# A fused attention and two-layer kernel: batch 4's first layer moved into block form, twenty operand sums moved to GpSimd, another opening order

## The chip, the cores and the metric

The kernel runs on one core of a Trainium2 chip. The metric is the device time in microseconds of one execution; lower is better. The core has a matrix engine (TensorE, "PE" in the profile, with its weight loads as "PEld"), a vector engine (VectorE, "DVE"), an activation engine (ScalarE, "ACT"), GpSimd ("POOL"), a queue engine (SyncE, "SP") and 16 DMA engines. Each engine works through its own instructions in order, and semaphores tie them together.

## What is computed

The input holds q, k and v of 8 batches, 12 heads, 448 positions and 64 features, and two weight matrices. Cut to what matters:

```python
scores = np.matmul(q, k.transpose(0, 1, 3, 2)) / np.sqrt(64)
attn   = np.maximum(scores, 0.0) ** 2 / 448
x      = np.matmul(attn, v)            # per batch and head
x      = x.transpose(0, 2, 1, 3).reshape(8 * 448, 768)
h      = x @ w_in                      # 3584 x 768 times 768 x 2048
g      = 0.5 * h * (1 + erf(h / sqrt(2)))
out    = g @ w_out                     # 3584 x 2048 times 2048 x 768
```

The attention has no softmax: the scores are cut at zero and squared. Its output, with the heads side by side, is the input of a two-layer network with an exact GELU.

## The kernel before

**Attention.** A batch is 21 steps: three groups of four heads (g) by seven key blocks (i). A step is four score matmuls on quarters of the array (line 659), then relu with the scale from PSUM into an SBUF tile a_sq (line 671 on ScalarE, or line 673 on VectorE), then the square in place on VectorE (line 680, which reads the same SBUF tile as both operands). After seven steps of a group comes an attention product of 28 matmuls (line 720), whose PSUM tile is cast to the bfloat16 tile xT in two copies (L436 on VectorE or L438 on ScalarE). Scores, products and the block form's accumulators share three PSUM tiles ("w"); a_sq has 14 buffers.

**First layer.** In its plain form (`add_f1`, line 772) a batch is 16 chunks, each of six matmuls of 448 columns into one PSUM tile ("f", two of them) and one GELU on ScalarE (line 782). In its block form (`add_blocks`, `add_block`, line 916) weights and input are cut into 2 x 2 blocks, and seven products take the place of eight: 168 matmuls of 224 columns. For this VectorE makes sums of the input blocks (xs, line 883) and, once, sums of the weight blocks (ws, `add_wsums`, line 841, of which one is written over a part of the weights in place), and combines the products in passes from PSUM (line 950), before GELUs (line 959). Batches 0 to 4 use the plain form, 5 to 7 the block form.

**Second layer.** Its output is made in 14 groups of 256 rows. Group 0 is plain (line 1181). Groups 1 to 13 (`add_group`) use the same seven-product scheme: four sums s1 to s4 of pieces of h (line 1067, 1,024 elements per partition, each with one buffer), then seven products p1, p6, p2, p7, p5, p4, p3 of eight matmuls each (line 1086), with passes on VectorE or ScalarE (line 1120, and copies by 436 and 438), and stores by SyncE. h lives in a ring of two batches.

**Loads and transposes.** q and k of batches 2 to 7 come in by GpSimd's DMA queue and are turned by DMA transposes that SyncE issues (line 585, nine per batch). GpSimd works through one list (`pool_q`): loads, and before the loads of a later batch a small gate copy (line 626) that waits until the transposes of an earlier one have landed. The output weights are loaded behind such a gate.

**The order.** The program is laid out by a planner (class `Scheduler`). It knows an estimated duration and latency for each operation, and places operations one by one. The opening is written out by hand as a list (`ORDER`): each word is an engine's letter and an operation's number. TensorE's later order is a list too (`pe_q`): the attention of batches 2 to 7, with first-layer chunks and second-layer products (`flow`) spread between its steps in proportion, and after the attention the list `end`, with the block form of batches 5 to 7 and groups 7 to 13. The planner may pull a layer chunk forward by its own estimate. Operations with two possible engines get one from the planner. The order of each engine is fixed in the program; on the chip, an engine whose operands are late holds all that stands behind them.

`add_av` makes the attention product and its two casts, `F1B` and `GROUPS` say which batches' chunks and which groups go beside which attention batch.

Of the kernel before, what the change touches and what calls it, by code (L numbers as in the profile page):

```python
# [12 lines left out]
B, H, S, D = 8, 12, 448, 64  # L13
# [8 lines left out]
G = H // 4  # L22
# [4 lines left out]
KF = FF // 128  # L27
# [14 lines left out]
X_BIAS = -0.2  # L42
# [8 lines left out]
SWITCH = 0.09  # L51
# [3 lines left out]
SUM_BIAS = -0.3  # L55
TSUM_BIAS = 0.2
LEADS = {}
SHARES = (1.3, 1.0, 1.0, 1.0, 1.0, 1.0)
LAST = 256
PASSES = 5  # L60
# [20 lines left out]


ORDER = """
G0 D13 A10 P11 D12 A16 G1 P17 G2 P14 D18 D15 P42 P39 G3 P19 D43 P33 D20 P36 D44 P21 P23 A40 G4
A34 D22 P51 D41 D24 A37 P54 P25 A55 D26 D35 P48 G5 A52 G6 D56 A49 P57 P69 D38 G7 P63 G8 A58 G9
A64 P66 D70 P45 D53 D59 D50 G117 P27 D65 A67 A28 A47 P31 A46 G118 D68 P60 P81 D32 P29 D62 A61
A82 D30 P78 G119 D71 P108 G120 D109 P75 A79 P93 D83 G121 A76 D80 P72 P90 A94 D73 G122 A74 P96
P84 D95 A91 P129 P102 D110 D130 P131 A85 P141 A97 D92 D132 A103 G123 P156 D98 P105 P111 P143
A142 D77 A106 P165 D112 D86 A157 D113 A166 D107 P99 A100 P87 A89 D104 D101 D88 A144 P114 G124
D167 D115 G125 P159 A116 P162 P133 P249 A163 A160 G126 A250 G127 D134 D158 P171 G128 D164 P168  # L90
P174 A169 P135 A136 P145 P195 G147 D172 P183 A146 D175 G148 D173 P186 A187 P241 P251 S228 A184
D176 D161 D196 P189 P180 A242 A252 G149 A190 D188 G150 G151 P198 D170 S231 G152 D181 P137 P139
P192 P177 D138 A199 G153 A193 D140 D191 P207 P222 A178 D185 D208 P243 A223 S230 A179 P204 A244
A205 P216 D197 G154 D182 G155 S229 D194 D200 D224 A217 P213 D206 P245 A214 A246 P259 P219 P210
P201 A220 D209 A211 A260 P261 A262 D218 P263 P253 A264 A254 P255 A256 P257 S232 P247 A202 D215
A203 D221 D212 A258 P225 A248 P265
"""


# [14 lines left out]
class Scheduler:  # L114
# [168 lines left out]
    def place(self, fixed):  # L283


        fixed = {e: list(v) for e, v in fixed.items()}
        inside = {id(o) for v in fixed.values() for o in v}

        names = {"P": "PE", "A": "ACT", "D": "DVE", "G": "POOL", "S": "SP"}
        gone = set()  # L290
        for word in ORDER.split():
            op, eng = self.open[int(word[1:])], names[word[0]]
            _, dur, lat = next(e for e in op.engines if e[0] == eng)
            self.commit(max(self.ready(op), self.free[eng]), op, eng, dur, lat)
            gone.add(id(op))
        fixed = {e: [o for o in v if id(o) not in gone] for e, v in fixed.items()}
        rest = [o for o in self.open if id(o) not in inside | gone]
        while rest or any(fixed.values()):
            by = {}
            for o in rest:  # L300
                for e in o.engines:
                    w = by.setdefault(e[0], [])
                    if len(w) < self.WINDOW:
                        w.append(o)
            tops = [self.pick(v, e) for e, v in by.items()]
            for e, v in fixed.items():
# [13 lines left out]
def kernel(  # L320
# [9 lines left out]
    nc = tc.nc  # L330
# [101 lines left out]
    V, A = nc.vector, nc.scalar  # L432
# [25 lines left out]
    F1, F2 = {}, {}  # L458
# [162 lines left out]
    def add_gate(b, g):  # L621


        def fn(e):
            n = (16 * g + 1) * KC
            nc.gpsimd.tensor_copy(gate, get_T(b)[0][:, n : n + 16 * KC : KC])  # L626

        deps = [Tq[b, g, c][0] for c in range(NC)] + [Tk[b, g, 0][0]]
        pool_q.append(sch.add((("POOL", 0.2, 0.3),), fn, deps))
# [75 lines left out]
    def add_av(blk, bias):  # L705
        b, g, _, half = blk
        blocks = [(b, g, i, half) for i in range(NK)]
        w = S if half is None else HS
        pav = []

        def fn(e_):
            pav.append(w_pp.tile([128, 2, NB], F32, tag="w", name="pav"))
            for i in range(NK):
                for j in range(2):
                    r = slice(64 * j, 64 * j + 64)
                    for e in range(2):
                        o2 = 64 * (e ^ j)
                        n, y = (i, e) if b < 2 else divmod(NK * e + i, 2)
                        _, box, o = SQ[blocks[n]]
                        nc.tensor.matmul(  # L720
                            pav[0][o2 : o2 + 64, e, :w],
                            vt[b][r, 2 * g + e, bass.ts(i, D)],
                            box["a2"][r, y, o : o + w],
                            start=(i == 0),
                            stop=(i == NK - 1),
                        )

        deps = list(dict.fromkeys(SQ[x][0] for x in blocks)) + ld_v[b, g]

        last = {id(SQ[x][1]): x for x in SQ}  # L730
        gone = sum(last[id(SQ[x][1])] == x for x in blocks)
        d = 7 * 0.19 * w / S
        op = sch.add(
            (("PE", d, d + 0.24),), fn, deps, mode="A", bias=bias + AV_BIAS, need=("w",),
            frees=("a",) * gone,
        )
        AV[b, g, half] = op

        def get_x():
            if b not in xT:  # L740
                p, tag = (vpool, "v") if b in (B - 3, B - 1) else (xpool, "xT")
                xT[b] = p.tile([128, HP, S], BF16, tag=tag, name="xT")
            return xT[b][:, 2 * g : 2 * g + 2, cols(half)]

        old = [o for (bb, *_), o in F1.items() if bb == b - 2]
        if b == B - 2:
            old = [o for (bb, *_), o in F1.items() if bb == b - 3]
        if b in (B - 3, B - 1):
            old = [o for (bb, *_), o in AV.items() if bb == b - 1]
        xs = X[b, g, half] = []  # L750
        for j in range(2):
            xs.append(
                sch.add(
                    e_copy(w, 1), lambda e, j=j: copy(e, get_x()[:, j], pav[0][:, j, :w]),
                    [op] + old, frees=("w",), joint=list(xs), bias=bias + X_BIAS,
                )
            )
        xs[0].joint = [xs[1]]
# [68 lines left out]
        return t[:, :, 128 * m : 128 * (m + m1 - m0)]  # L827

    WS = {}

    def add_wsums(after, done):

# [25 lines left out]
    def add_blocks(b):  # L858
# [16 lines left out]

            return fn

        gone = [o for (bb, *_), o in QK.items() if bb == (B - 2 if b == B - 3 else B - 1)]

        def xsum(n, op, l, r, deps):  # L880
            return sch.add(
# [11 lines left out]
        for m4 in (0, M1 // 2):  # L893
            bank, todo = {}, []
            for y in range(2):
                ms = range(m4 + 2 * y, m4 + 2 * y + 2)
                todo.append(add_block(b, m4, y, ms, bank, x, t, TS, xs, old, half))
            for p in zip(*todo):
                atoms += [(0.58, o) for o in p]
            for name in ("a", "b", "c"):  # L900
                u, v = bank["end", name]
                u.joint, v.joint = [v], [u]
# [144 lines left out]
            queue.pop(0).dma_start(to[k, p0 : p0 + m, c], src[y : y + m, c])  # L1047
            j += m

    def add_group(g):  # L1050

        rows = [range(256 * g + 128 * x, 256 * g + 128 * x + 128) for x in range(2)]
        bs = sorted({r // S for t in rows for r in (t[0], t[-1])})
# [10 lines left out]
        def sum_op(n, op, a, b, deps):  # L1064
            def fn(e):
                box["s", n] = spool.tile([128, K2, 128], BF16, tag=f"s{n}", name=f"s{n}_sb")
                V.tensor_tensor(box["s", n], a(), b(), op=op)

            o = sch.add(
                (("DVE", 0.69, 0.8),), fn, deps, need=(f"s{n}",), bias=SUM_BIAS  # L1070
            )
            mine.append(o)
            return o

# [229 lines left out]
        add_load(2, g, g + 1)  # L1304
    add_steps(steps(1), ATT1_BIAS, True)
    add_T_dma(2, [[]] * 9)
    add_gate(2, G - 1)
    add_wout(0)
    add_wout(1)
    add_wout(2)  # L1310
    for m in range(0, HALF_M, 2):
        add_f1(0, m, 1, bias=F1B_BIAS)
    for m in range(HALF_M, KF):
# [20 lines left out]
    def at(b, n):  # L1334
        return [at_slot(b, n)]
# [1 line left out]
    for g in range(G):  # L1337
        add_load(3, g, g + 1)
    add_v(3, 0, G)
    flow, plans = [], {}  # L1340
    F1B = {2: 1, 3: 2, 4: 3, 5: 4}
    GROUPS = {2: (1,), 3: (2, 3), 4: (4, 5), 5: (6,)}
    for b in range(2, B):
        add_steps(steps(b), dve=True)
# [8 lines left out]
        if b + 1 < B:  # L1353
# [3 lines left out]
            if b + 2 < B:  # L1357
# [1 line left out]
                    add_gate(b + 1, g)  # L1359
                    add_load(b + 2, g, g + 1)  # L1360
                add_v(b + 2, 0, G)
        flow += [y for g in GROUPS.get(b, ()) for y in add_group(g)]
    add_wsums(at(B - 1, 1), [F1[B - 4, m, None] for m in range(KF)])

    def woven(x, y):

# [5 lines left out]
                out.append(y.pop(0))  # L1372
        return out + y

    end = woven(add_blocks(B - 3), add_group(7))
    end += add_group(8)
    end += woven(add_blocks(B - 2), add_group(9))
    g10 = add_group(10)
# [54 lines left out]
```

## Time and profile before

Three runs of the kernel took 370.72, 372.26 and 372.67 us; the median is 372.26. The profiled execution took 372.0 us, its span from the first to the last instruction is 370.2 us.

| engine | busy us | share of the span |
|---|---|---|
| PE | 359.3 | 97% |
| DVE | 279.0 | 75% |
| ACT | 205.5 | 55% |
| POOL | 63.4 | 17% |

The granted TensorE clock is 0.995 of full speed on average. The attention of batch 0 begins about 7 us after the start, that of batch 2 at 67, and the last attention product (batch 7) is at 252 us. From there to 365 us TensorE works on the block form and on groups 7 to 13.

In the profile's rows, "L680 DVE TENSOR_TENSOR a_sq<-a_sq 128x896 ... x88 | 51.8, 619 | 2.3" reads: line 680 of the kernel, on VectorE, writes tile a_sq from tile a_sq, 128 partitions by 896 elements, 88 times; busy 51.8 us in all, 619 ns each; the engine was idle 2.3 us just before them. A timeline row gives start, length, engine, line, operation, tiles and count. The rows of a timeline that have a count over one are merged instructions of the same kind in a row. Reported durations overlap slightly from one instruction to the next, so a pace is best taken from start to start.

### The profile page before, as it was taken

What the parts mean: (1) busy time and instruction counts of PE and PEld (TensorE: products, weight loads), DVE (VectorE), ACT (ScalarE), POOL (GpSimd) and SP (SyncE); (2) the same over time, 40 slices, a digit from 0 to 9 for tenths busy, and PEclk for the clock granted to TensorE, in tenths of its full rate; (3) what the DMA queues carried; (4) which work ended last, traced back from release to release, by engine and by line L of the source; (5) the groups of instructions that cost most, each with busy time, mean ns of one, the idle gap of its engine ahead of it and who ended that gap; (6) DMA issues with size and microseconds to landing.
All of it is one profiled execution on the core that took longest, in us unless ns stands there. A gap on an engine that the chain in (4) does not pass through costs nothing.

```text
span 370.2 us, 8463 instructions
## 1 busy us (share of the span) xinstructions
PE 359.3 (97%) x3557; PEld 222.2 (60%) x3557; DVE 279.0 (75%) x477; ACT 205.5 (55%) x315; POOL 63.4 (17%) x101
## 2 busy tenths in 40 slices
PE   7789999999999999999999999999999999999995
PEld 6566645455554455544455544457876897688663
DVE  3799930579997688997689978999878558755862
ACT  4798974664667745877755687854540353045200
POOL 8666301530023034004014000000000000000000
PEclk9899999999999999999999999999999999999999
DMA  9999997999999999999999993002002301210223
GB/s 171 195 201 203 202 200 115 161 203 196 200 140 228 164 160 177 171 153 210 164 156 183 201 180 76 2 0 88 2 0 87 88 0 43 90 41 2 85 85 87
DMA packets 89269, 47.27 MB, mean 128 GB/s; under 512 B 55312, under 2 KB 85776, under 8 KB 89232
## 3 DMA queue, kind: packets, MB, share of 16 engines
q0 software_dynamic: 32912, 22.47, 44.9%
q1 hardware_dynamic: 55952, 23.76, 36.3%
q8 instruction: 28, 0.46, 0.6%
q10 hardware_dynamic: 368, 0.51, 0.4%
q14 instruction: 9, 0.07, 0.1%
HBM read 45.61 MB, written 11.01 MB: 153 GB/s over the span
## 4 chain that ended last, share of the span: by engine, by line
PE 92%; ACT 3%; DVE 2%; DMA 1%; issue 0%; DVEq 0%
PE pso L1086 32%; PE psh L772 25%; PE pb L916 13%; PE ps L659 9%; PE pav L720 8%; ACT a_sq L671 3%; PE pso L1181 3%; DMA q<-in_q_dram 1%; PE tp L558 1%; DVE part L950 1%; PE tp L530 1%; DVE a_sq L680 0%; DVE xT L436 0%; ACT xT L438 0%; DVE kT L436 0%; DVE xs L883 0%
## 5 line engine op out<-in xcount | busy, mean ns | idle before, releaser
L671 ACT ACTIVATE a_sq<-ps 128x896 bf16<-128x896 f32 x139 | 120.0, 920 | 36.9 <-PE ps L659 36.9
L680 DVE TENSOR_TENSOR a_sq<-a_sq 128x896 bf16<-128x896 bf16 (+1 forms) x169 | 98.0, 616 | 3.0 <-ACT a_sq L671 2.0
L772 PE MATMUL psh<-xT,win_sb 128*128 128x448 bf16 (+1 forms) x516 | 96.4, 340 | 0.0
L772 PEld LDWEIGHTS <-win_sb 128*128 128x128 bf16 x516 | 47.9, 98 | 45.0 <-issue 9.1
L782 ACT ACTIVATE h_sb<-psh 128x448 bf16<-128x448 f32 x80 | 44.0, 550 | 26.9 <-PE psh L772 26.8
L1086 PEld LDWEIGHTS <-s_sb 128*128 128x128 bf16 x424 | 40.4, 98 | 27.5 <-issue 3.1
L673 DVE TENSOR_SCALAR a_sq<-ps 128x896 bf16<-128x896 f32 (+1 forms) x30 | 31.7, 1058 | 27.9 <-PE ps L659 27.9
L659 PE MATMUL ps<-qT,kT 64*64 64x448 bf16 (+1 forms) x756 | 48.0, 336 | 3.3 <-ACT a_sq L671 3.1
L950 DVE TENSOR_TENSOR part<-pb,part 128x448 f32<-128x448 f32 x60 | 34.6, 619 | 20.7 <-PE pb L916 20.7
L1086 PEld LDWEIGHTS <-h_sb 128*128 128x128 bf16 x312 | 29.9, 98 | 21.3 <-issue 2.8
L1086 PE MATMUL pso<-wout_sb,s_sb 128*128 128x384 bf16 (+2 forms) x216 | 38.1, 320 | 0.1
L1086 PE MATMUL pso<-wout_sb,h_sb 128*128 128x384 bf16 x208 | 38.1, 326 | 0.0
L1086 PE MATMUL pso<-t_sb,s_sb 128*128 128x384 bf16 x208 | 38.1, 326 | 0.0
L720 PE MATMUL pav<-a_sq,v_sb 64*64 64x448 bf16 (+1 forms) x756 | 37.3, 337 | 0.4 <-ACT a_sq L671 0.4
L659 PEld LDWEIGHTS <-kT 64*64 64x64 bf16 x756 | 18.3, 105 | 25.5 <-issue 19.5
L959 ACT ACTIVATE h_sb<-part 128x448 bf16<-128x448 f32 x36 | 20.1, 578 | 20.2 <-DVE part L950 20.0
L720 PEld LDWEIGHTS <-v_sb 64*64 64x64 bf16 x756 | 21.8, 110 | 11.9 <-issue 1.8
L916 PEld LDWEIGHTS <-win_sb 128*128 128x128 bf16 x288 | 27.6, 98 | 2.3 <-issue 0.4
L436 DVE CAST xT<-pav 128x448 bf16<-128x448 f32 (+1 forms) x38 | 21.1, 587 | 10.3 <-PE pav L720 9.7
L1120 DVE TENSOR_TENSOR osb<-pso,p_sb 128x384 f32<-128x384 f32 x39 | 21.7, 555 | 8.3 <-PE pso L1086 6.1
L626 POOL COPY gate<-qT 128x16 bf16<-128x16 bf16 x13 | 4.0, 304 | 110.1 <-DMA qT<-nq 110.1
L916 PEld LDWEIGHTS <-ws 128*128 128x128 bf16 x216 | 20.7, 98 | 0.0
(58 smaller groups left out, 291.3 us busy)
## 6 DMA issues: line engine op xcount, KB each, us to landing
nk<-in_k_dram POOLq DMA_DIRECT2D x23, 224.0 KB, 6.5
nq<-in_q_dram POOLq DMA_DIRECT2D x21, 224.0 KB, 9.1
v_sb<-in_v_dram POOLq DMA_DIRECT2D x5, 672.0 KB, 13.9
out_dram<-osb SPq DMA_DIRECT2D x8, 336.0 KB, 3.8
v_sb<-in_v_dram POOLq DMA_DIRECT2D x9, 224.0 KB, 8.5
out_dram<-osb SPq DMA_DIRECT2D x7, 288.0 KB, 3.4
out_dram<-osb SPq DMA_DIRECT2D x8, 240.0 KB, 3.1
win_sb<-in_moe_w_in_dram POOLq DMA_DIRECT2D x8, 192.0 KB, 8.6
```

The source lines that it names most:

```text
L436: V.tensor_copy(dst, src)
L659: nc.tensor.matmul(ps[64 * j : 64 * j + 64, e, x * w : x * w + w], kT[r, g, i * 128 + 64 * j : i * 128 + 64 * j + 64], moving, start=True, ...
L671: A.activation(ar, ps, AF.Relu, scale=c_att)
L673: V.tensor_scalar(ar, ps, c_att, 0.0, op0=mybir.AluOpType.mult, op1=mybir.AluOpType.max,)
L680: V.tensor_mul(box["a2"][:, :, :used], ar, ar)
L720: nc.tensor.matmul(pav[0][o2 : o2 + 64, e, :w], vt[b][r, 2 * g + e, bass.ts(i, D)], box["a2"][r, y, o : o + w], start=(i == 0), stop=(i == ...
L772: nc.tensor.matmul(ph[:, x * n : x * n + n], win_sb[:, kd, bass.ts(m + x, 128)], xT[b][:, kd, c], start=(kd == 0), stop=(kd == KD - 1),)
L782: A.activation(h_ring()[:, m : m + nm, o + c.start : o + c.stop], box[0][:, :S].rearrange("p (x n) -> p x n", x=nm), AF.Gelu,)
L916: nc.tensor.matmul(bank[name][:, y, z * HS : z * HS + HS], w[:, k, bass.ts(mm, 128)], right()[:, k], start=first and k == 0 and z == 0, st ...
L950: V.tensor_add(get(to), ps(name), get(other))
L1086: nc.tensor.matmul(box[bank][:, n0:n1], left()[:, kf], right()[:, kf, n0:n1], start=bool(need) and kf == 0, stop=kf == K2 - 1, skip_group_ ...
L1120: V.tensor_add(out()[:, n0:n1], box[bank][:, n0:n1], other()[:, n0:n1])
```

## The change

Three parts, which the planner's layout ties together:

1. Batch 4's first layer is made in block form too. Its 16 plain chunks leave the list beside attention batch 5, and its blocks come first in the list `end`, with no second-layer group woven in; the blocks of batch 5 and group 7 follow, as before. The tiles of the input sums take a buffer of the transposed keys of batch 6, and batch 6's own input sums follow in that buffer. The weight sums wait for the plain chunks of batch 3, the last plain ones now, and no longer for those of batch 4.
2. The four sums of each of groups 2 to 6, 20 in all, are made by GpSimd. They are put into its list: those of groups 2 and 3 after the loads of batch 5, those of groups 4, 5 and 6 after the loads of batch 7, which are its last.
3. The opening's list is another one. The planner now counts the time of a change between kinds of matmul while it follows that list, and takes the second cast of an attention product as dependent on the first. The loads of the output weights stand behind gates that wait for the first and the second third of batch 2's transposes, and the loads of batch 3 behind that for the last third; before, all stood behind the gate for the last third.

```diff
+POOLED = {2: 3, 3: 3, 4: 5, 5: 5, 6: 5}
...
 ORDER = """
-G0 D13 A10 P11 D12 A16 G1 P17 G2 P14 D18 D15 P42 P39 G3 P19 D43 P33 D20 P36 D44 P21 P23 A40 G4
...
+A10 P11 D13 A16 D12 P17 D18 P14 G0 P42 A15 G1 P39 A40 G2 P19 D43 G3 D44 P21 A22 P33 D20 P36 G4
...
@@ place
-            self.commit(max(self.ready(op), self.free[eng]), op, eng, dur, lat)
+            free = self.free[eng]
+            if eng == "PE" and self.mode not in (None, op.mode):
+                free += SWITCH
+            self.commit(max(self.ready(op), free), op, eng, dur, lat)
@@ add_av
-                    [op] + old, frees=("w",), joint=list(xs), bias=bias + X_BIAS,
+                    [op] + old + xs, frees=("w",), joint=list(xs), bias=bias + X_BIAS,
@@ add_blocks
-        gone = [o for (bb, *_), o in QK.items() if bb == (B - 2 if b == B - 3 else B - 1)]
+        gone = [o for (bb, *_), o in QK.items() if bb == (B - 2 if b == B - 4 else B - 1)]
+        if b == B - 2:
+            gone += blocks[B - 4]
...
+                blocks.setdefault(b, []).extend(p)
@@ add_group
-    def add_group(g):
+    def add_group(g, pooled=None):
...
-                V.tensor_tensor(box["s", n], a(), b(), op=op)
-
-            o = sch.add(
-                (("DVE", 0.69, 0.8),), fn, deps, need=(f"s{n}",), bias=SUM_BIAS
-            )
+                (V if pooled is None else nc.gpsimd).tensor_tensor(box["s", n], a(), b(), op=op)
+
+            eng = ("DVE", 0.69, 0.8) if pooled is None else ("POOL", 2.3, 2.5)
+            o = sch.add((eng,), fn, deps, need=(f"s{n}",), bias=SUM_BIAS)
+            if pooled is not None:
+                pooled.append(o)
@@ the main list
-    add_gate(2, G - 1)
+    add_gate(2, 0)
     add_wout(0)
     add_wout(1)
+    add_gate(2, 1)
     add_wout(2)
+    add_gate(2, 2)
...
-    flow, plans = [], {}
-    F1B = {2: 1, 3: 2, 4: 3, 5: 4}
+    flow, plans, held = [], {}, {}
+    F1B = {2: 1, 3: 2, 4: 3}
...
-        flow += [y for g in GROUPS.get(b, ()) for y in add_group(g)]
-    add_wsums(at(B - 1, 1), [F1[B - 4, m, None] for m in range(KF)])
+        flow += [y for g in GROUPS.get(b, ()) for y in add_group(g, held.setdefault(g, []) if g in POOLED else None)]
+        for g in POOLED:
+            if g in held and POOLED[g] == b:
+                pool_q.extend(held[g])
+    add_wsums(at(B - 1, 1), [F1[B - 5, m, None] for m in range(KF)])
...
-    end = woven(add_blocks(B - 3), add_group(7))
+    end = list(add_blocks(B - 4))
+    end += woven(add_blocks(B - 3), add_group(7))
```

More of the change, by code (lines that the diff above doesn't have):

```diff
@@ L83 @@
 ORDER = """
-G0 D13 A10 P11 D12 A16 G1 P17 G2 P14 D18 D15 P42 P39 G3 P19 D43 P33 D20 P36 D44 P21 P23 A40 G4
[L85 to L96, printed above, removed]
+A10 P11 D13 A16 D12 P17 D18 P14 G0 P42 A15 G1 P39 A40 G2 P19 D43 G3 D44 P21 A22 P33 D20 P36 G4
+P54 G5 P25 A37 P23 A55 G6 P51 D34 P48 A24 A49 D26 D35 D56 D41 D38 A52 P69 D70 G7 P57 P63 A58
+D53 P45 D50 P66 G8 G9 D59 A64 A46 P27 P31 D28 G117 D32 A67 D65 D68 A47 G118 P60 P78 G119 A61
+P29 D30 G120 P81 A79 A82 D62 G121 G122 P93 A94 D71 P108 P84 A85 P75 D109 A76 D83 D80 P72 P90
+D73 P129 D95 P105 A74 G123 P102 A91 D130 A106 P131 D86 D77 G124 D132 P141 D92 A103 P111 P96
+G125 A112 P165 P143 A97 D104 P156 D107 A166 A157 P87 D113 D98 P99 D110 D88 G126 A142 D89 P114
+P174 P133 D100 G127 A101 A175 D115 D116 P159 A144 P168 D134 G128 P171 D169 A160 P135 D172 D173
+D170 A136 G147 P251 P192 D193 P186 P162 A252 P145 D176 A163 A146 P243 P253 P180 P195 A187 A244
+P198 P137 A254 G148 D164 D158 P139 G149 G150 A181 D167 G151 A199 D161 P183 D196 A184 P177 D138
+D140 D188 G152 P189 P219 P245 P247 D194 A178 A190 S231 A220 D185 A179 P207 P216 A246 S229 D182
+P213 D191 D197 P261 A248 A208 S232 P263 S228 D200 A214 P222 D217 P204 D221 D209 P201 D215 A262
+A223 A264 P210 A211 P265 G153 S230 A266 P259 A260 P249 P255 D218 D205 A202 A250 A203 P257 D224
+G154 A256 D206 D212 P225 P267 G155 A258
 """
@@ L829 @@
     WS = {}
+    blocks = {}
     def add_wsums(after, done):
```

## The prediction

> **What bounds the kernel now.** I read the page first. The parts on busy time and on slices:
>
> ```profile
> PE 359.3 (97%) x3557; PEld 222.2 (60%) x3557; DVE 279.0 (75%) x477; ACT 205.5 (55%) x315; POOL 63.4 (17%) x101
> ...
> PE   7789999999999999999999999999999999999995
> ...
> DVE  3799930579997688997689978999878558755862
> ...
> POOL 8666301530023034004014000000000000000000
> ```
>
> TensorE is busy in every slice but the first three and the last: about 11 of 370.2 us are idle, and the chain that ended last is 92% PE. So every microsecond of matmul taken away counts, provided that the engines feeding it keep up. VectorE is the one near its limit: 9 tenths in many slices of the attention. GpSimd is nearly free, and after 200 us empty.
>
> Then the timeline of PE, for the pace of the two forms of the first layer (start, us, line, count):
>
> ```profile
> 48.37 6.98 PE L772 MATMUL psh<-xT,win_sb 128*128 128x448 bf16 x36
> 55.28 0.95 PE L720 MATMUL pav<-a_sq,v_sb 64*64 64x448 bf16 x16
> ...
> 306.72 1.31 PE L916 MATMUL pb<-xs,win_sb 128*128 128x224 bf16 x12
> 307.87 1.31 PE L916 MATMUL pb<-xT,ws 128*128 128x224 bf16 x12
> ```
>
> From start to start, 36 plain matmuls take 6.91 us (0.192 each) and 12 block ones 1.15 us (0.0958 each), with no gap between groups.
>
> Then VectorE's groups between 105 and 230 us, where groups 2 to 6 of the second layer lie, with the engines' busy time in that stretch:
>
> ```profile
> L680 DVE TENSOR_TENSOR a_sq<-a_sq 128x896 bf16<-128x896 bf16 x88 | 51.8, 619 | 2.3 <-ACT a_sq L671 1.5
> L673 DVE TENSOR_SCALAR a_sq<-ps 128x896 bf16<-128x896 f32 x14 | 15.3, 1092 | 12.6 <-PE ps L659 12.6
> L436 DVE CAST xT<-pav 128x448 bf16<-128x448 f32 x25 | 14.4, 616 | 1.2 <-PE pav L720 1.1
> L1067 DVE TENSOR_TENSOR s_sb<-h_sb 128x1024 bf16<-128x1024 bf16 x10 | 6.8, 683 | 0.0
> ...
> 105.00:230.00 125.00, 124.88 (x1172) 63.43 (x1171) 105.28 (x177) 84.89 (x120) 22.48 (x37) 1.00 1.24 172
> ```
>
> The stretch's columns are PE, weight loads, DVE, ACT, POOL. VectorE is busy 105.3 of 125 us. Its most frequent operation is the square, which reads two operands from SBUF; relu, the casts to xT and the passes read PSUM.
>
> Last, how late the squares may be (timelines of DVE and PE around an attention product of the last batch):
>
> ```profile
> 231.47 1.27 DVE L680 TENSOR_TENSOR a_sq<-a_sq 128x896 bf16<-128x896 bf16 x2
> ...
> 233.18 1.49 PE L720 MATMUL pav<-a_sq,v_sb 64*64 64x448 bf16 x28
> ```
>
> The last square ends at 232.74, the product starts at 233.18: 0.44 us to spare. Over the 18 products of batches 2 to 7 the same difference is 0.2 to 2.4 us, 1.05 on average; they come every 10 us.
>
> **The Trainium skill.** "GPSIMD Engine Reference", section 3.1, gives about 2.6 cycles per element at 1.2 GHz for a two-input tensor_tensor. Estimate for 1,024 elements: 2.2 us. The trace of before has no such operation on GpSimd. "SBUF — State Buffer", section "Who interferes with whom", says that a VectorE instruction with two SBUF inputs contends with a GpSimd instruction that reads SBUF, and that whichever starts first holds the shared port for its whole instruction. The trace agrees for one direction. Two gate copies on GpSimd with what VectorE did meanwhile:
>
> ```profile
> 143.52 0.61 POOL L626 COPY gate<-qT 128x16 bf16<-128x16 bf16 x1 [9.36 <-DMA qT<-nq]
> ...
> 143.44 0.62 DVE L680 TENSOR_TENSOR a_sq<-a_sq 128x896 bf16<-128x896 bf16 x1
> ...
> 169.56 0.21 POOL L626 COPY gate<-qT 128x16 bf16<-128x16 bf16 x1 [0.89 <-DMA qT<-nq]
> ...
> 168.90 1.09 DVE L673 TENSOR_SCALAR a_sq<-ps 128x896 bf16<-128x896 f32 x1 [1.29 <-PE ps L659]
> ```
>
> Under a square the copy takes 0.61 us and ends 0.07 after the square; under a relu from PSUM it takes 0.21. Seven of the 13 copies fall under a two-input operation, and each ends 0.06 to 0.08 after it; the other six take 0.2. The opposite direction, VectorE held by GpSimd, no run here shows yet.
>
> **The change, part by part**, against the profiled execution's own 372.0 us (span 370.2, so 1.8 around it; the median of the runs shown is 372.26, 0.3 above, which I neglect).
>
> *Batch 4 in block form.* Removed: 16 chunks of 6, 96 x 0.192 = 18.4 us of PE. Added behind the attention: 168 matmuls (504 in three batches now) x 0.0958 = 16.1. Sum **-2.3 us**, on the path, as PE is full there. Added on DVE: 20 passes of 0.62 and 4 sums xs of 0.5, 14.4 us beside 16.1 of PE; the first blocks now have no second-layer group woven in. Now VectorE spends 7.2 of 10 us in 260 to 270 and PE doesn't wait; each bank's pass has a pair of products (1.15 us) as cover, against 0.62. Taken as 0; if the weight sums (8 x 0.95) come late too, VectorE passes 16.1 us and it costs up to 2. ACT: 16 GELUs as before and 4 copies (0.53), hidden, since it is busy 5 of 10 us there.
>
> *Attention made shorter.* PE loses 18.4 us of filler, so the same squares, relus and casts must be done in 18.4 us less. In the stretch above: DVE 105.3 less the 20 sums on GpSimd (start to start 0.6 each, 12) is 93 in 106.6 us, 87% against 84% before. ACT: 84.9 less 16 GELUs x 0.55 is 76 in 106.6, 71%. Loads and transposes per batch must also be done in some 26 instead of 30 us; SP's transposes of one batch started 22 us after those of the batch before at the fastest (113.6, then 135.6), so they fit.
>
> *The 20 sums on GpSimd.* Each takes 2.2 us by the page's price; bounds: 1.1 (the 128-element affine select takes 0.31 and the 16-element copy 0.20, so about 1 ns an element) and 2.8 (a 0.6 us wait for a square in front). For 20 it is 45 us in which GpSimd reads SBUF. What does VectorE do meanwhile? It goes on until the next two-input operation stands at its head. Without the sums 92 of 157 of its operations in the stretch are of that kind (88 squares and 4 sums xs and ws), 59%; so it gets through 0.41/0.59 = 0.7 operations of about 0.7 us, 0.5 us, and stands for the remaining 1.7. Times 20: 35 us (0 if it isn't held at all). Against it: the 13.6 us that VectorE has idle in the stretch, and the slack of about 1 us in front of an attention product, once for each of the five groups, 5 us. Remainder 35 - 13.6 - 5 = 17 us of PE waiting. I take **+12**: the planner sees a lighter VectorE, may place relus on ACT (14 of 1.09 us are on VectorE in the stretch, ACT has 30 us idle; five moved give 5 us). Ends: -0 and +22.
> What waits in VectorE's queue behind a held square is all of it: the relu and the two casts that give PSUM tiles back to the next scores, the passes that free a bank for the next product, and the last square of an attention product; PE's order is fixed, so it waits too.
> What waits behind the sums in GpSimd's queue: those of groups 2 and 3 stand ahead of the gates of batch 5 and the loads of batch 6. The sums of group 3 need the buffers that group 2's products give back, near the end of batch 4. So these loads, at 147 to 172 us now, start about one third of a batch or more later; they have the length of batch 5 (26 us) until their first scores. 4.1 MB at 200 GB/s is 20 us, transposes follow by thirds: hidden, with some 8 us to spare. Behind the sums of groups 4 to 6 stands nothing.
>
> *Gates and output weights.* The first gate now waits for a third of batch 2's transposes, so the weight loads (63.8 now) go out some 10 us earlier and share the DMA engines with the other transposes (all done at 61; the first scores of batch 2, at 67, need the first third alone). Two more gate copies, 0.2 us each on a GpSimd that waits there: 0; if the later thirds slip by more than some 10 us, up to +1.
>
> *Opening and planner.* The order lists engine by engine nearly the same work; PE is idle 4.5 us between 6 and 30 us, in waits of 0.4 us for a relu. The planner now counts mode switches there and puts the second cast behind the first. Bounds -1.5 and +1.5; taken as 0.
>
> Sum: 372.0 - 2.3 + 12 = **381.7, so 382 us**.
>
> **Rivals.**
> *A, forecast: VectorE is held* (above), 376 to 391. For it: the copies of 0.61 us. Chance 0.62.
> *B, held but absorbed*: the held time is under (13.6 + 5)/20 = 0.9 us per sum or a little more, because GpSimd gives the port back early or the sums fall where VectorE casts. Then 371 to 376, mostly 373. Chance 0.14.
> *C, the other side: VectorE isn't held by GpSimd's reads, or under 0.9 us a sum, and the shorter matmuls arrive whole*: 372.0 - 2.3 = 369.7, with the opening's bounds 368.3 to 371. For it: PE idles nowhere else, and 84 to 87% of VectorE was enough. Against: the copies show that reads exclude each other. Chance 0.17.
> *D, GpSimd's queue*: the loads of batch 6 or a sum are late and PE waits for DMA or for GpSimd itself. Between p5 of one group and p6 of the next lie p4, p3 and p1, 3.9 us and attention; two sums take 4.4. At 2 us for each of the three such seams and up to 8 us for late transposes, 372.0 - 2.3 + 6 to 14 gives 376 to 384. Chance 0.07, as the cause on its own.
>
> **From these to the numbers.** About 0.5% (1.9 us) is what a measurement of this kernel can tell from no change. Faster, under 370.4: C, 0.17 plus a little of B, 0.18. Within: part of B and the edge of C, 0.09. Slower: A, D and half of B, 0.73. The range 369.3 to 390 takes in half of C, all of B and D and nine tenths of A, some 0.83; A alone is 376 to 391.
>
> **What would show it.** Squares on line 680 longer than 0.63 us or gaps before them, while a sum of 2 us or more runs on GpSimd; PE waiting for VectorE between 110 and 235 us, where it has no wait now, in steps at groups 2 to 6; the end of attention at about 251 - 18 + 12 = 245 us, and the tail after it 16 us longer than now at the same pace. C would show the end of attention at 233 and squares at 0.62. Wrong would make it: sums of 1.1 us; a planner that empties VectorE at those places; squares that go on under a sum.

## The result and the profile after

The changed kernel takes 401.6 us (median of four runs, 397.2 to 409.1), the kernel before 372.2 beside it: a ratio of 1.076, with a 95% interval of 1.066 to 1.085 (the ratio leaves out the run of 409.1 us, which fell in a slower state). The forecast was 382 us, with a range up to 390. The sign was right, the size wrong by a factor of three: +29.4 us instead of +10.

The page after, parts on busy time and slices (the profiled execution's span is 399.3 us):

```profile
PE 366.6 (92%) x3629; PEld 231.3 (58%) x3629; DVE 305.4 (76%) x484; ACT 204.3 (51%) x316; POOL 110.2 (28%) x123
...
PE   8699999999999839799979879899999999999995
...
DVE  3999814898987708998799979998979766765862
...
POOL 8755212401123096901390817200000000000000
PEclk9999999999999969899989969999999999999999
```

TensorE, full in every slice before, now has seven holes between slices 14 and 26, and four of them (15, 17, 21 and 23) lie where GpSimd's row has an 8 or a 9. Its busy time went up by 7.3 us although its work went down by 2.3; the row of the granted clock says why: it has 6 and 8 there, where before it had 9.

Where in the run the time goes can be read from PE's timeline: the start of each batch's first score matmul, of the first block-form product, and the end (us).

| kernel | b=2 | b=3 | b=4 | b=5 | b=6 | b=7 | first block product | end |
|---|---|---|---|---|---|---|---|---|
| before | 67.1 | 102.6 | 132.7 | 162.8 | 192.0 | 222.9 | 251.6 | 370.2 |
| after | 65.0 | 97.6 | 125.5 | 167.0 | 194.2 | 225.8 | 263.5 | 399.3 |

Up to batch 4 the change is 7 us ahead, as a thinner filler should make it. Then batch 4 takes 41.5 instead of 30 us, batch 7 37.6 instead of 29. By the first block product it is 11.8 us behind, where 18.4 ahead was the plan: 30.2 us are lost in the attention. What follows takes 135.9 instead of 118.6 us, 17.3 more, against 16.1 for the matmuls added there.

The three largest of PE's waits, none of which was there before (us in total, times, longest):

```profile
PE pso L1095 <- POOL s_sb L1075: 8.4, 1, 8.4
PE pav L724 <- DVE a_sq L684: 7.4, 7, 1.9
PE pso L1095 <- DVE osb L1129: 3.9, 3, 2.3
```

And one place of the second kind in full, group 5's sums in batch 7 (timelines of GpSimd, VectorE and TensorE):

```profile
223.50 2.39 POOL L1075 TENSOR_TENSOR s_sb<-s_sb,h_sb 128x1024 bf16<-128x1024 bf16 x1
225.84 2.50 POOL L1075 TENSOR_TENSOR s_sb<-h_sb 128x1024 bf16<-128x1024 bf16 x1
228.31 2.49 POOL L1075 TENSOR_TENSOR s_sb<-h_sb,s_sb 128x1024 bf16<-128x1024 bf16 x1
...
224.29 1.07 DVE L677 TENSOR_SCALAR a_sq<-ps 128x896 bf16<-128x896 f32 x1
225.28 6.00 DVE L684 TENSOR_TENSOR a_sq<-a_sq 128x896 bf16<-128x896 bf16 x3
231.20 0.54 DVE L1129 TENSOR_TENSOR osb<-pso,osb 128x384 f32<-128x384 f32 x1
...
228.88 0.57 PE L724 MATMUL pav<-a_sq,v_sb 64*64 64x448 bf16 x8 [1.75 <-DVE a_sq L684]
231.33 0.89 PE L724 MATMUL pav<-a_sq,v_sb 64*64 64x448 bf16 x7 [1.88 <-DVE a_sq L684]
...
233.69 2.74 PE L1095 MATMUL pso<-t_sb,s_sb 128*128 128x384 bf16 x8
```

Three squares, which take 1.7 us in a row with no sum beside them, take 6.0: while GpSimd sums, VectorE's square stands, gets in between two sums, and the next one stands again. The relu from PSUM at 224.29, under a sum too, takes its usual 1.07. PE waits for the squares, and the product that follows takes 2.74 us instead of 1.46: half clock.

### The profile page after: what moved, and what is told of

The parts are those of the page before. It is cut to its first block, busy times and chain, and to the rows that moved or that the text cites. A ratio compares the mean times of both kernels' runs of the same rounds, so it can differ in the third digit from the quotient of the medians.

```text
span 399.3 us, 8659 instructions
## 1 busy us (share of the span) xinstructions
PE 366.6 (92%) x3629; PEld 231.3 (58%) x3629; DVE 305.4 (76%) x484; ACT 204.3 (51%) x316; POOL 110.2 (28%) x123
## 4 chain that ended last, share of the span: by engine, by line
PE 66%; DVE 15%; SPq 6%; ACT 5%; DMA 4%; issue 2%; POOL 2%; DVEq 0%; POOLq 0%; ACTq 0%
PE pso L1095 24%; PE pb L924 14%; PE psh L776 14%; DVE a_sq L684 8%; SPq L589 6%; PE ps L663 6%; PE pav L724 5%; DMA qT<-nq 4%; ACT a_sq L675 4%; DVE part L958 2%; DVE osb L1129 1%; DVE a_sq L677 1%; PE spin L1256 1%; DVE ws L846 1%; POOL s_sb L1075 1%
## 5 line engine op out<-in xcount | busy, mean ns | idle before, releaser
L675 ACT ACTIVATE a_sq<-ps 128x896 bf16<-128x896 f32 x131 | 113.4, 918 | 59.6 <-PE ps L663 59.4
L684 DVE TENSOR_TENSOR a_sq<-a_sq 128x896 bf16<-128x896 bf16 (+1 forms) x169 | 116.8, 733 | 3.0 <-ACT a_sq L675 2.3
L776 PE MATMUL psh<-xT,win_sb 128*128 128x448 bf16 (+1 forms) x420 | 77.9, 339 | 0.0
L958 DVE TENSOR_TENSOR part<-pb,part 128x448 f32<-128x448 f32 x80 | 46.1, 620 | 22.2 <-PE pb L924 22.2
L776 PEld LDWEIGHTS <-win_sb 128*128 128x128 bf16 x420 | 39.1, 98 | 36.6 <-issue 9.1
L677 DVE TENSOR_SCALAR a_sq<-ps 128x896 bf16<-128x896 f32 (+1 forms) x38 | 40.8, 1075 | 22.9 <-PE ps L663 22.8
L1095 PE MATMUL pso<-t_sb,s_sb 128*128 128x384 bf16 x208 | 41.5, 347 | 10.1 <-POOL s_sb L1075 8.4
L786 ACT ACTIVATE h_sb<-psh 128x448 bf16<-128x448 f32 x64 | 35.0, 550 | 23.2 <-PE psh L776 23.1
L967 ACT ACTIVATE h_sb<-part 128x448 bf16<-128x448 f32 x48 | 26.7, 578 | 25.4 <-DVE part L958 25.1
L1075 POOL TENSOR_TENSOR s_sb<-h_sb 128x1024 bf16<-128x1024 bf16 x10 | 23.5, 2350 | 26.9 <-PE pso L1095 26.8
L924 PEld LDWEIGHTS <-ws 128*128 128x128 bf16 x288 | 27.6, 98 | 0.4 <-issue 0.4
## 6 DMA issues: line engine op xcount, KB each, us to landing
win_sb<-in_moe_w_in_dram POOLq DMA_DIRECT2D x8, 192.0 KB, 8.5
```

The source lines that it names most:

```text
L675: A.activation(ar, ps, AF.Relu, scale=c_att)
L677: V.tensor_scalar(ar, ps, c_att, 0.0, op0=mybir.AluOpType.mult, op1=mybir.AluOpType.max,)
L684: V.tensor_mul(box["a2"][:, :, :used], ar, ar)
L776: nc.tensor.matmul(ph[:, x * n : x * n + n], win_sb[:, kd, bass.ts(m + x, 128)], xT[b][:, kd, c], start=(kd == 0), stop=(kd == KD - 1),)
L786: A.activation(h_ring()[:, m : m + nm, o + c.start : o + c.stop], box[0][:, :S].rearrange("p (x n) -> p x n", x=nm), AF.Gelu,)
L924: nc.tensor.matmul(bank[name][:, y, z * HS : z * HS + HS], w[:, k, bass.ts(mm, 128)], right()[:, k], start=first and k == 0 and z == 0, st ...
```

## The experiments

**The sums back on VectorE.** Edit:

```diff
-POOLED = {2: 3, 3: 3, 4: 5, 5: 5, 6: 5}
+POOLED = {}
```

> The changed kernel with all second-layer sums on VectorE again; block form of batch 4 and the new opening stay. Theory 'hold' (GpSimd's reads of the sums keep VectorE's two-operand instructions waiting) and theory 'queue' (the sums come late because of what stands before them in GpSimd's list) both expect the whole loss gone: 366 to 370 us, that is 372.2 less 2.3 for the block form and about 2 for the opening; no square over 0.65 us. Theory 'thin filler' (with 18 us of matmul gone from beside the attention VectorE can't follow, wherever the sums are) expects 380 us or more.

382.9 us, ratio 1.028 (1.021 to 1.035). So taking the sums back gains 18.7 us, and the rest, which was forecast as a gain of 2.3, costs 10.8. The size that "thin filler" named came, but not its mechanism. Timelines of VectorE, TensorE and SyncE of this kernel:

```profile
166.62 0.56 DVE L1129 TENSOR_TENSOR osb<-pso,p_sb 128x384 f32<-128x384 f32 x1 [6.98 <-DMA out_dram<-osb]
...
167.23 2.72 PE L1095 MATMUL pso<-t_sb,h_sb 128*128 128x384 bf16 x8 [5.55 <-DVE osb L1129]
...
152.78 3.42 SPq L589 DMA_TRANSPOSE kT<-nk  x1
156.26 4.60 SPq L589 DMA_TRANSPOSE qT<-nq  x2
160.97 2.41 SPq L1055 DMA_DIRECT2D out_dram<-osb  x4
```

VectorE isn't overloaded here, it stands idle for 7 us. It wants an output tile (there are three), and the store that frees it goes out at 161, behind transposes of batch 5 that take SyncE up to 3.4 us each, though group 2's output was complete at 151.7. From 165.4 us on, still within PE's wait, the clock is at half for 6.8 us: the 16 matmuls after the wait take 5.1 us instead of 2.6.

**The three parts alone, on the kernel before.** The sums alone (group 4's ahead of the last v load, since the planner has no solution otherwise; group 7's, on VectorE, are planned after them):

```diff
+POOLED = {2: 3, 3: 3, 4: 5, 5: 5, 6: 5}
...
+                if g == 4:
+                    pool_q[-1:-1] = held[g]
+                else:
+                    pool_q.extend(held[g])
```

> The kernel before with only the 20 sums of groups 2 to 6 on GpSimd (group 4's stand before the last v load, as the plan has no solution otherwise; group 7's are planned after them). Hold: 20 us of longer squares as in the changed kernel, some of it absorbed as the filler is 18 us thicker: 385 to 400 us. Queue: only the one wait of 8 us at group 2, if the gates of batch 4 are as late: 380. Thin filler: 372 to 376.

411.2 us, ratio 1.100 (1.091 to 1.108), above what any theory said. In its profiled execution, the longest of the four with 414.2 us, PE waited 13.0 and 11.7 us for the second sum of groups 2 and 4, both behind gates in GpSimd's list, and squares were 17 us longer in all. The sums cost more here than in the changed kernel, so the parts don't add up. That the lateness of GpSimd's list depends on where the plan puts the groups fits these waits, but wasn't tested by itself.

The opening, the planner's two corrections and the gates alone:

```diff
+            if eng == "PE" and self.mode not in (None, op.mode):
+                free += SWITCH
...
+                    [op] + old + xs, frees=("w",), joint=list(xs), bias=bias + X_BIAS,
...
+    add_gate(2, 0)
     add_wout(0)
     add_wout(1)
+    add_gate(2, 1)
     add_wout(2)
+    add_gate(2, 2)
```

> The kernel before with only the new opening list, the two planner corrections and the three gates. The first scores of batch 2 came 2.0 us earlier in the changed kernel. If that lead is carried to the end: 370.2 us. If it is given back, because a later wait sets the pace: 371.5 to 373.

372.7 us, ratio 1.0005 (0.998 to 1.003): nothing, as forecast. In its trace the first scores of batch 2 come at 66.5 instead of 67.1 us and the first block product at 251.7 instead of 251.6. The 2 us of lead in the changed kernel are not the opening's alone.

Batch 4 in block form alone:

```diff
-    F1B = {2: 1, 3: 2, 4: 3, 5: 4}
+    F1B = {2: 1, 3: 2, 4: 3}
...
+    end = list(add_blocks(B - 4))
+    end += woven(add_blocks(B - 3), add_group(7))
```

> The kernel before with only batch 4 in block form behind the attention. Saving of matmul time carried whole: 369.9 us (372.2 less 2.3). Thin filler: VectorE at its limit beside the shorter attention, PE waits in 105 to 235 us, 375 us or more.

384.5 us, ratio 1.032 (1.028 to 1.037). A gain of 0.6% on paper costs 3%. The longest wait is of the same kind as above: PE 5.8 us behind VectorE, VectorE 6.7 us behind a store.

**What in the sums costs the time?** First the place in the list: group 2's sums ahead of the gates of batch 4.

```diff
+                if g == 2:
+                    pool_q[early:early] = held[g]     # early: before batch 4's gates
+                else:
+                    pool_q.extend(held[g])
```

> The changed kernel with group 2's four sums in GpSimd's list ahead of the gates of batch 4, not behind its loads. Queue: PE's wait of 8.4 us for the second sum of group 2, and about 2.5 us of slow clock after it, go: 390 us. If something else stands at the same place (the stores behind the transposes, as in the kernel with the sums back on VectorE, 5.6 us) part of it returns: 393 to 398. Hold: the 20 us of longer squares stay, in any case.

399.9 us, ratio 1.074 (1.070 to 1.079): not to be told from the change itself. The wait of 8.4 us is gone, but squares are now 27.6 us longer in all than at their usual 618 ns, instead of 19.9, because these sums fall beside a busy VectorE; in the changed kernel they fell into a time in which PE and VectorE stood still anyway. PE's waits for VectorE grew from 11.9 to 17.2 us. So this run doesn't tell what the wait of 8.4 us costs by itself.

Then the reads: GpSimd writes the same tiles and reads nothing.

```diff
-                (V if pooled is None else nc.gpsimd).tensor_tensor(box["s", n], a(), b(), op=op)
+                    for _ in range(2):
+                        nc.gpsimd.memset(box["s", n], 0.0)
```

> The changed kernel with each of the 20 sums on GpSimd replaced by two memsets of the same tile: GpSimd writes, and reads nothing from SBUF. The sums of groups 2 to 6 are left out, so that the output isn't the reference's. Hold: squares go back to 0.62 us, none over 0.65, although GpSimd is about as busy; the losses after 155 us go and the time falls to 380 to 388 us. If VectorE was slowed by GpSimd's activity as such, or by late sums: squares stay long, or the time stays over 395.

382.1 us, ratio 1.025 (1.021 to 1.030). The squares (line 684; nanoseconds least, median, longest) of the change:

```profile
L684 DVE TENSOR_TENSOR a_sq<-a_sq x169: 384/618/2542, 8.2 to 264.2; 128x896 bf16<-128x896 bf16 x167, 128x448 bf16<-128x448 bf16 x2
```

and, with the memsets, the squares and the memsets themselves:

```profile
L684 DVE TENSOR_TENSOR a_sq<-a_sq x169: 383/618/634, 8.3 to 244.8; 128x896 bf16<-128x896 bf16 x167, 128x448 bf16<-128x448 bf16 x2
...
L1079 POOL MEMSET s_sb<- x40: 951/951/977, 143.0 to 232.8; 128x1024 bf16 x40
```

GpSimd is nearly as busy as with the sums (99.9 us against 110.2, with 40 memsets of 0.95 us), its list has the same order, and PE still waits 5.9 us once for GpSimd. But no square is longer than 634 ns, and the time is that of the sums back on VectorE (1.025 against 1.028, overlapping intervals). It is the reads that cost: 401.6 - 382.1 = 19.5 us. What is left above before has two waits of PE in it that before had not, the 5.9 us for GpSimd and 2.8 us for transposes, and none for a store.

Last, half of the reads: a copy of one operand in place of the sum.

```diff
-                (V if pooled is None else nc.gpsimd).tensor_tensor(box["s", n], a(), b(), op=op)
+                if pooled is None:
+                    V.tensor_tensor(box["s", n], a(), b(), op=op)
+                else:
+                    nc.gpsimd.tensor_copy(box["s", n], a())
```

> The changed kernel with each of the 20 sums on GpSimd replaced by a copy of its first operand (the sums are left out, so the output isn't the reference's): GpSimd reads one operand instead of two and is busy for a shorter time, 1.0 to 1.2 us. Hold: squares are still stretched, by up to the length of the copy, in all less than half of 20 us; 384 to 392 us. If only two-operand reads hold VectorE: squares at 0.62 and 380 to 382 us, as with memsets.

383.7 us, ratio 1.029 (1.022 to 1.035). The copies (15 of the 20; the other five read another tile) and the squares:

```profile
L1078 POOL COPY s_sb<-h_sb x15: 1035/1056/1851, 144.1 to 233.6; 128x1024 bf16<-128x1024 bf16 x15
...
L684 DVE TENSOR_TENSOR a_sq<-a_sq x169: 381/616/1461, 8.4 to 247.1; 128x896 bf16<-128x896 bf16 x167, 128x448 bf16<-128x448 bf16 x2
```

A copy takes 1.05 us against 2.1 to 2.5 for a sum. Squares are still held, the longest to 1.46 us instead of 2.54, but all overruns add up to 5.1 us instead of 19.9, and the slack absorbs these: the time can't be told from that with none. So the hold is not worth a fixed sum per microsecond; there is a part that is free, and the sums lie beyond it.

**What in the block form costs 10.8 us?** All of what follows has the sums on VectorE (the first experiment's kernel, 382.9 us). First the queue: the stores of groups 2 and 3 are issued by ScalarE, past SyncE's transposes.

```diff
+        q = nc.scalar if g in (2, 3) else nc.sync
         if g < NG - 1:
-            sch.add((("SP", 0.6, 2.8),), store(1, full, [nc.sync] * 2), [c22, c21], frees=("osb",))
+            sch.add((("SP", 0.6, 2.8),), store(1, full, [q] * 2), [c22, c21], frees=("osb",))
...
```

> The kernel with all sums on VectorE, and the stores of groups 2 and 3 issued by ScalarE's queue and not by SyncE's, where they stood behind the transposes of batch 5. If these stores caused VectorE's wait of 7.0 us for an output tile (5.6 us of PE, and about 2.5 of slow clock after it): 374 to 376 us. If the tile is late for another reason (a DMA that is slow by itself): 382 to 384, with the wait still there.

394.0 us, ratio 1.061 (1.056 to 1.066): 11 us worse, not better. ScalarE's timeline at that place:

```profile
157.16 2.13 ACTq L1055 DMA_DIRECT2D out_dram<-osb  x2
...
159.35 0.92 ACT L675 ACTIVATE a_sq<-ps 128x896 bf16<-128x896 f32 x1 [9.44 <-DMA qT<-nq]
```

ScalarE, which had nothing to do with the transposes, now waits 9.4 us for one (17.8 in two such places), and the relus behind it with it; PE waits 15.8 us for ScalarE. The semaphores in the trace tell why: in this program the DMAs of SyncE and ScalarE, transposes among them, take eight semaphores in turn, and each waits, ahead of its issue, until the DMA that had its semaphore before has landed. ScalarE's store at 157.16 waited so for a transpose issued by SyncE at 146.7 us, which landed at 157.1. With the stores on SyncE it was another wait: there the semaphore of the store at 160.97 had been free since 145.2 us, and the store went out as soon as SyncE had issued the transposes ahead of it, at 160.9. So the move exchanged a wait for a turn in the queue for one for a landing, and put the relus behind it.

Then the stores of groups 2 and 3 are left out.

```diff
+        keep = (lambda fn: lambda e: None) if g in (2, 3) else (lambda fn: fn)
         if g < NG - 1:
-            sch.add((("SP", 0.6, 2.8),), store(1, full, [nc.sync] * 2), [c22, c21], frees=("osb",))
+            sch.add((("SP", 0.6, 2.8),), keep(store(1, full, [nc.sync] * 2)), [c22, c21], frees=("osb",))
...
```

> The kernel with all sums on VectorE, with the stores of groups 2 and 3 left out (512 rows of the output aren't written; everything else is as it was). If VectorE's wait of 7.0 us is for these stores, which themselves wait for transposes to land, it goes, with PE's 5.6 us and the slow clock behind it: 373 to 376 us. If PE then waits at the same place for something else (scores of batch 5 or 6 for their transposes): 380 or more. What remains over 370 is VectorE at the first block-form products.

374.7 us, ratio 1.007 (1.004 to 1.010). 8.2 of the 10.8 us hang on these eight DMAs (with the stores goes their traffic, which this run doesn't part from the wait). 2.6 us remain above before, in place of 2.3 below. The first block product starts at 237.4 us, 14.2 ahead of before (18.4 planned: PE still waits for transposes of q).

```profile
PE ps L663 <- DMA qT<-nq: 3.5, 2, 2.8
```

This profiled execution took 377.4 us, 2.7 above the median, so these waits may be shorter as a rule. What follows takes 138.2 us, 19.6 more than before (16.1 planned; 17.3 in the changed kernel). The first 20 us of that part, as windows (length, PE, weight loads, DVE, ACT, POOL busy, granted clock, DMA share, GB/s), of before and of this kernel:

```profile
250.00:270.00 20.00, 20.00 (x199) 16.89 (x197) 16.18 (x30) 9.87 (x19) 0.00 (x0) 1.00 0.14 41
```

```profile
240.00:260.00 20.00, 17.54 (x176) 16.34 (x173) 18.27 (x32) 9.20 (x19) 0.00 (x0) 1.00 0.00 1
```

PE lost 2.5 of 20 us here and none before; VectorE is at 18.3 instead of 16.2. Seven of the eight weight sums (0.95 us each) fall into 239 to 256 us, on top of the passes.

Is it VectorE's load there? Twelve of the 20 passes of that batch work on 32 columns only, the rest of their work is left out:

```diff
-                    V.tensor_add(get(to), ps(name), get(other))
+                    n = 32 if b == B - 4 and to == other else S
+                    V.tensor_add(get(to)[:, :n], ps(name)[:, :n], get(other)[:, :n])
```

> The kernel with all sums on VectorE and without the stores of groups 2 and 3, in which 12 of the 20 passes of batch 4's blocks also work on 32 columns instead of 448 (so most of these blocks' combination is left out). It takes some 5 us from VectorE behind the attention and nothing from PE. If VectorE is what makes PE wait at the first blocks (2.2 us of waits there, the tail 3.5 us longer than the matmuls): 371 to 372.5 us. If the tail is longer for another reason: 374 to 375, as without it.

373.8 us, ratio 1.005 (1.003 to 1.007): 0.9 us less, with intervals that overlap. In its trace PE waits 1.3 us in the first 20 us of that part instead of 2.5, and the part takes 136.8 us instead of 138.2. So VectorE's load there explains some of the excess, not all of it. The other runs give a hint: in the changed kernel, and in those with memsets and copies, four of the eight weight sums and not seven start after the first block product; PE waits 0.5 us there, and the part takes 135.9 us. These plans differ in more than that, and the weight sums' place was not tried by itself, so the rest of the tail's excess stays open.

Two ways to a real repair. The stores by GpSimd, whose completion counters are others:

```diff
+        by, q = (("POOL", 1.4, 4.2), nc.gpsimd) if g in (2, 3) else (("SP", 0.6, 2.8), nc.sync)
         if g < NG - 1:
-            sch.add((("SP", 0.6, 2.8),), store(1, full, [nc.sync] * 2), [c22, c21], frees=("osb",))
+            sch.add((by,), store(1, full, [q] * 2), [c22, c21], frees=("osb",))
...
```

> As the kernel with all sums on VectorE, but the stores of groups 2 and 3 go by GpSimd's own DMA queue, planned there. If what held them is that a store issued by SyncE or ScalarE has to wait for earlier transposes, GpSimd's queue is free of it: 373 to 377 us. If the stores are slow because the DMA engines are busy, or now stand behind a gate in GpSimd's list: 380 to 386.

386.3 us, ratio 1.031 (1.025 to 1.037): no gain. The store goes out at 159.8 us, 1.2 us ahead of where SyncE sent it, but still 9 us after group 2's output was complete (150.5), behind gates in GpSimd's list that wait for the same batch's transposes; VectorE waits 8.0 us for it, PE 6.6. And the planner's costs of a transpose, 1.4 us on SyncE and 3.6 until it is there, closer to what the trace shows:

```diff
-T_STEP = 1.4
-T_TIME = 3.6
+T_STEP = 2.2
+T_TIME = 7.0
```

> The kernel with all sums on VectorE, planned with the transposes' measured cost: 2.2 us of SyncE each instead of 1.4, landing after 7.0 us instead of 3.6. If the stores came to stand behind the transposes because the planner took these for quick, they move ahead of them or the transposes start earlier: 373 to 376 us, as with the stores left out. If the DMA engines can't carry this attention any faster: 380 or more.

378.2 us, ratio 1.017 (1.014 to 1.021): 4.7 us back.

```profile
157.52 3.20 SPq L1055 DMA_DIRECT2D out_dram<-osb  x4
...
162.82 0.56 DVE L1129 TENSOR_TENSOR osb<-pso,p_sb 128x384 f32<-128x384 f32 x1 [4.36 <-DMA out_dram<-osb]
...
163.43 1.46 PE L1095 MATMUL pso<-t_sb,h_sb 128*128 128x384 bf16 x8 [2.94 <-DVE osb L1129]
```

The store goes out at 157.5 instead of 161, 7 us after the output was complete instead of 9, VectorE waits 4.4 us instead of 7.0, PE 2.9 instead of 5.6, and the half clock after that wait is gone (eight matmuls in 1.46 us instead of 2.72). It is the best of the kernels that do the whole work with block form, and still slower than before.

## Why the prediction was right or wrong

In the order in which the experiments took the parts away, the 29.4 us are: opening and gates 0; block form with the opening 10.8; sums 18.7. The forecast had 0, -2.3 and +12. The split holds for this order alone: added singly to the kernel before, the sums cost 39.1 us and the block form 12.5, together far more than 29.4.

The changed kernel's own trace gives the loss by waits. PE waits 8.4 us for GpSimd, 11.9 for VectorE and 1.5 for transposes, and is busy for 7.3 us more; that makes 29.1 us, which is by how much its span is longer than that of before. Its other waits are about as before.

*Batch 4 in block form: wrong.* The step that failed is "-2.3 us, on the path, as PE is full there". The arithmetic on PE held (less filler ahead, 16 us more behind), but the path that it shortened was not PE's alone. The prediction asked of SyncE's queue whether the transposes fit into 26 us a batch; it did not ask what stands behind them. With the sums on VectorE the stores stand there: one that goes out 9 us after its data is complete stops VectorE, which has three output tiles, and then PE. Leaving these stores out gives back 8.2 us, and planning with the transposes' measured length, all stores made, 4.7. In the changed kernel no wait for a store shows; at the same place PE waits 8.4 us for group 2's sums, which stand in GpSimd's list behind gates that wait for transposes. In both kernels it is work that stands behind transposes. The prediction also took the loads and transposes as hidden once they fit: without the stores PE still waits up to 3.5 us for transposes. For the tail, "taken as 0 … up to 2" was enough in the changed kernel (17.3 us more against 16.1) and too low with the sums on VectorE (19.6, with PE waiting 2.5 us in its first 20); the prediction's own figures, 14.4 and 8 x 0.95 us of VectorE beside 16.1 of PE, gave 5.9 and not 2. The end of the attention was to be at 245 and came at 263.5.

*The sums on GpSimd: right in the mechanism, with its terms mis-sized.* Squares above 0.63 us under a sum, in steps at groups 2 to 6, and PE waiting for VectorE were what forecast A named, and they came (up to 2.54 us). The experiment that writes without reading shows that the reads do it. The gross of 35 us was 19.9, 1.0 us for each sum: VectorE isn't held for 1.7 us of each sum as if every sum found a square; the two alternate one by one, and the sums share in the loss (2.5 us each when they alternate with squares, 2.1 alone). The cover of 18.6 us was more than twice too high: of 19.9 us of overrun about 12 came out as PE's waits on VectorE (7.4 for squares, 3.9 for output tiles, 0.6 elsewhere), so about 8 were absorbed. (35 less this cover is 16.4, not 17; that counts for little.) The idle time of VectorE lies where it waits for PE's scores, and a square that is late there makes the next scores late in turn. Nor did the planner move five relus to ScalarE, for which the forecast took off 5 us; it put eight more on VectorE (38 on line 677, 30 on line 673 before). And a term was missing: waits leave a slow clock behind. The windows of the changed kernel have, for one of the stretches,

```profile
230.00:240.00 10.00, 8.09 (x43) 3.44 (x46) 7.32 (x12) 1.73 (x2) 0.80 (x1) 0.66 0.13 39
```

a granted clock of 0.66. There are four such spells in the attention, of 6.8, 3.4, 3.4 and 6.8 us, against two, of 3.4 and 6.8 us, in the kernel that only writes; PE is 6.4 us busier than in that kernel (366.6 against 360.2), with the same matmuls. 12 and 6.4 make 18.4 of the 19.5 us.

*Rivals B and C* (absorbed; not held) fell with the squares; B is what happens with copies, whose 5.1 us of overrun cost nothing that could be measured. *Rival D* had a real place in the changed kernel: PE waited 8.4 us for group 2's sums, which stand behind gates of batch 4, not in the seams that D named. It isn't what the reads cost, since the kernel that only writes has it too (5.9 us) and takes 382.1 us; it belongs to the rest above before, in the place of the store's wait. To put these sums ahead of the gates was no repair: that took the wait away and brought 5.3 us more of waits for VectorE, and the time stayed.

*Opening and gates: right.* 0.0, and no slip of the later thirds.

*The range.* It took in errors of every named term, but the term that held the 10.8 us was given -2.3, with at most 2 us to be lost behind it.

The Trainium skill's "SBUF — State Buffer", section "Who interferes with whom", says that a GpSimd read and a two-input VectorE operation exclude each other and that GpSimd's writes alone don't. The runs agree in both: 2.54 us under a sum, 0.634 at most under a memset; and an operation with PSUM as source, the relu of 1.07, isn't touched. "TensorE: Matmul & The Clock Gate", section "HAM oscillation — how this bites in real kernels", warns of idle gaps over about 3.4 us. In the first experiment one of 5.6 us brought 6.8 us of half clock, which agrees. In batch 7 of the changed kernel two waits of 1.75 and 1.88 us, 2.5 us apart, were enough for as much. In the kernel with memsets a single wait of 2.60 us was followed by 3.4 us of half clock, while waits of 2.75 us (stores left out) and 2.94 us (true transposes) were followed by none. Here the measurement decides: waits under 3.4 us can be enough, and their length alone doesn't tell.

## What to carry to other kernels

When a change shortens a full engine's work, walk down every queue that feeds it or empties it, not for whether its load fits but for what stands behind each long item: here a store behind transposes, worth 8 us, sat in front of a three-deep buffer. Work that moves from VectorE to GpSimd is not off VectorE's hands if it reads SBUF beside VectorE's two-input operations: here 20 sums cost 19.5 us, and 20 copies, which read half as much, nothing that could be measured. A wait of PE can cost more than its length, so price the half clock after it too.

## What the runs showed of the hardware

GpSimd's sum and VectorE's square take turns, one square between two sums, so that three squares took 6.0 us instead of 1.7; a weight sum on VectorE took 1.95 us instead of 0.95 in the same way. For 128 x 1,024 bf16 GpSimd takes 0.95 us for a memset, 1.05 for a copy, 2.1 for a sum alone and 2.4 to 2.5 for one that alternates with squares. In the changed kernel half-clock spells at PE's waits lasted 3.4 or 6.8 us, also after two waits of less than 2 us close together; a single wait of 2.94 us elsewhere brought none. In the first experiment's kernel a DMA transpose took SyncE 1.2 to 6.4 us to issue, 2.0 in the median. ScalarE stood idle for 9.4 us while stores in its queue waited for transposes that SyncE had issued.
